# Block-causal attention with a SwiGLU layer on one core: the first microseconds rearranged

## The chip, the cores and the metric

The kernel runs on one core of a Trainium2 chip. The metric is device time in microseconds from the first to the last instruction of one execution, with what the launch adds around it; the median of several executions is compared. The engines are called PE (TensorE, with PEld for its weight loads), DVE (VectorE), ACT (ScalarE), POOL (GpSimd) and SP (SyncE, which here only issues transfers).

## The reference

Attention over 8 batches, 8 heads, 576 positions and a head dimension of 64, where a query sees the keys of its own block of 64 and of earlier blocks; the heads are then put side by side and go through a gated layer of widths 512, 1536 and 512. The weights of the layer arrive as 64-bit numbers.

```python
scores = scale * np.matmul(q, k.transpose(0, 1, 3, 2))
mask = block_i >= block_j                      # blocks of 64 positions
scores = np.where(mask, scores, -1000000000.0)
scores = scores - np.max(scores, axis=-1, keepdims=True)
attn = np.exp(scores)
attn = attn / (np.sum(attn, axis=-1, keepdims=True) + 1e-09)
x = np.matmul(attn, v)     # then as 4608 rows of 512
g = x @ w_gate
out = (g * (1.0 / (1.0 + np.exp(-g))) * (x @ w_val)) @ w_out
```

## The kernel before

The work is cut into tasks. `add(engine, cost, rank, fn, after, bufs)` records one: the engine, a planned cost, a rank, the function that emits its instructions, the tasks that it waits for and the buffers that it uses. `in_order()` then plays the tasks through a small model of five engines: whenever an engine is free, the ready task of lowest rank whose buffers are free goes next. The resulting list is emitted one task after the other, so each engine's program is that list in that order; what an instruction really waits for are its data and its buffers.

**Attention.** Scores are held with the keys on the partitions. Batches 0 and 1 are "early": each is cut into queries 0 to 255 and 256 to 575 (`FIRST`), and the eight heads go in four pairs. For a pair: `load_qk` brings q (SP) and k (ACT's queue for the very first four loads), `transposes` turn them on PE (L374) with `ident`, the 128x128 matrix of one, into the PSUM tiles `gv` or `at`; ACT copies them into `parts` (L382); `products` make the scores on PE (L400); ACT hides the unseen blocks (L441) and copies for the maximum (L444); DVE takes the maximum over key chunks into `mx` (L574); POOL reduces it over the partitions with PARTITION_ALL_REDUCE (L578); DVE subtracts it into `sc` (L602); ACT takes the exponent (L606); PE multiplies with `v` and with `ones` for the sums (L646). For the first 256 queries of batch 0, "tile 0", DVE inverts the sums (L673 to L677), multiplies (L680) and makes the low part (L297) of `xhl`, the input of the layer. There are four such inputs, one a pair.

**The layer.** The 4608 rows go in tiles of 256. `feed_forward` makes gate and value products on PE (L959 to L961; three products of high and low parts) into `gv`, and the down products (L1050 to L1052) into `po`. The weights come as pairs of 32-bit words: `weight(i, kind)` loads one block of gate, value or output weights (L812) into one of five `wo` buffers; ACT (L827) and DVE (L832, L836, L841) build 32-bit numbers from the words, and ACT and DVE split them into a high and a low part (L846, L849). There are 12 blocks of three kinds. The rank of a block's load is that of its other tasks: `R = 2.5 + i / 100.0 if i < 2 else 4.0 + i / 10.0`.

**Buffers.** PSUM has two `at`, two `gv` and one `po`; a task waits until the buffer that it writes is released. POOL fills the tiles of `v` and the tail of the keys in `parts` with zeros (L233, L211), and SP's first load into such a tile waits for that. `scratch` is the first `ob` tile, which ACT later uses for the weights' words.

**The matrix of one before:** on DVE, a row counting up is doubled in length seven times, turned for the partition's number, and compared (L271 to L279).

Of the kernel before, what the change touches and what calls it, by code (L numbers as in the profile page):

```python
# [9 lines left out]
I32 = mybir.dt.int32  # L10
AF = mybir.ActivationFunctionType
ALU = mybir.AluOpType
# [5 lines left out]
def kernel(  # L18
# [17 lines left out]
    nc = tc.nc  # L36
    B, H, S, D = q.shape
# [18 lines left out]
    MIXED = (0, 0, 0, 1, 1, 0, 1, 0, 1, 0, 1, 1)  # L56

    FINE = 4

    PATIENCE = 10.0  # L60

# [54 lines left out]
    class Task:  # L116
        def __init__(self, engine, cost, rank, fn, after, bufs, port, mode):
            self.engine, self.cost, self.rank, self.fn = engine, cost, rank, fn
            self.bufs, self.waits, self.next, self.ready = bufs, 0, [], 0.0
            self.moves, self.port, self.mode = 0.0, port, mode  # L120

            self.prev = None

    tasks = []

# [15 lines left out]
    def act_us(n):  # L141
        return 0.08 + n * 0.000833
# [4 lines left out]
    def mm_us(*ns):  # L147
        return sum(n / 2400.0 + 0.0145 for n in ns)


    def pair_us(*ns):
        return sum(n / 600.0 + 0.01 for n in ns)
# [113 lines left out]
            tiles_of(tag, place, variant)  # L266


    scratch = tiles_of("ob", 0)[0]
    count, mine = scratch[:, 0:P], scratch[:, P : P + 32]  # L270
    nc.vector.memset(count[:, 0:1], 0.0)  # L271
    for i in range(7):
        n = 2**i
        nc.vector.tensor_scalar(count[:, n : 2 * n], count[:, 0:n], float(n), None, ALU.add)
    nc.vector.transpose(mine, count[:, 0:32])
    for i in range(1, P // 32):
        rows = slice(32 * i, 32 * (i + 1))
        nc.vector.tensor_scalar(mine[rows, 0:1], mine[rows, 0:1], 32.0 * i, None, ALU.add)
    nc.vector.tensor_scalar(ident, count, mine[:, 0:1], None, ALU.is_equal)  # L279

    x_d = dram.tile([DM, NT], F32, name="x_d")
    s_d = dram.tile([H, NT], F32, name="s_d")
# [22 lines left out]
    def attention(R, b, h, a, e, early, bufs, lane):  # L305
# [35 lines left out]
        def plain_scores():  # L341
# [21 lines left out]
            for i in range(2):  # L363
                ps = Buf("gv") if whole else Buf("at", also=banks)
                nb = len(blocks[i])
                per = nb if nb < 6 else 3

                def turned(ps=ps):
                    return ps[0].rearrange("p (x n) -> p x n", x=1) if whole else ps[0]

                def transposes(i=i, turned=turned, per=per):
                    for m, c in enumerate(blocks[i]):
                        o = m % per * TB
                        nc.tensor.transpose(  # L374
                            turned()[:, m // per, o : o + TB],
                            qk[0][:TB, lane * 3 + c, 2 * i * D : 2 * (i + 1) * D],
                            ident[:TB, :TB],
                        )

                def out_of_psum(i=i, turned=turned, nb=nb, per=per):  # L380
                    o = L + blocks[i][0] * TB
                    nc.scalar.mul(  # L382
                        prt[i][:, o : o + nb * TB].rearrange("p (x n) -> p x n", x=nb // per),
                        turned()[:, 0 : nb // per, 0 : per * TB],
                        1.0 if i else SCALE,
                    )

                tr = add("PE", 0.083 * nb, R, transposes, [ld[i]], [qk, ps, prt])
                ready.append(add("ACT", act_us(nb * TB), R, out_of_psum, [tr], [ps, prt]))

            for visit in visits:
# [16 lines left out]

                ws = [w for parts in visit for _, _, w in parts]
                pr = add("PE", pair_us(*ws), Q, products, ready, [*both, prt, sc], mode="rows")  # L410
                for parts, ps in zip(visit, both):
                    gw = sum(w for _, _, w in parts)
                    mixed = [(c, sum(w for _, _, w in parts[:i])) for i, (c, qs, _) in enumerate(parts) if qs == c * P]
# [216 lines left out]
                    in_=v[b, h : h + 2, nf * P : e].rearrange("h p d -> p h d"),  # L630
                )

        vl = dma(R, 3e5, load_v, [], [vt], 3 if e % P else 2)
        segs = [s for s in ((0, 2 * P), (2 * P, S)) if a <= s[0] and s[1] <= e]
        ends = []
        direct = b == 0
# [146 lines left out]
    def weight(i, kind):  # L783
# [5 lines left out]


        R = 2.5 + i / 100.0 if i < 2 else 4.0 + i / 10.0
        raw = Buf("wo", "raw")
        away = AWAY.get(i) if kind == 2 else None
        wo = Buf("wo", "out") if kind == 2 and not away else None
# [16 lines left out]
                src = words(w_out)[i * P : (i + 1) * P, :].rearrange("p (n m) -> p n m", n=1)  # L811
            nc.sync.dma_start(out=view, in_=src)  # L812

        t = chain["w"] = dma(R, 5e5, load, [chain["w"]], [raw])
        bufs = [raw, wo] if wo else [raw]

        def words_of(j):
# [116 lines left out]
    def feed_forward(j, t0, w, xs):  # L934
# [41 lines left out]
        for i in range(0, NFC, 2):  # L976
# [65 lines left out]
            for piece in pieces:  # L1042
# [12 lines left out]
                after = [a, *(took[y][0] for y in ys), *{ends[m] for m in ms}]  # L1055
                bufs = [acc, hh, *(took[y][1] for y in ys if took[y][1])]
                t = add("PE", mm_us(DM, DM, DM) * len(piece), rank(i), products, after, bufs)
                for m in ms:
                    ends[m] = t
                if j >= FINE:  # L1060
# [21 lines left out]
    def with_v(rank):  # L1082
        us, products, after, bufs = zip(*(next(pair) for pair in at_work))
        t = add(
            "PE", sum(us), rank, lambda: [f() for f in products], sum(after, []), sum(bufs, []), mode="columns"
        )
        for pair in at_work:
            try:
                pair.send(t)
            except StopIteration:  # L1090
                pass
        at_work.clear()
# [44 lines left out]
    def in_order():  # L1137
# [42 lines left out]
        while events:  # L1180
# [3 lines left out]
            for e in engines:  # L1184
# [20 lines left out]
                order.append(t)  # L1205
                end = now + t.cost
                if e == "PE":
                    end, mode, last = end + 0.2 * (t.mode != mode), t.mode, t
                idle[e] = end
                heapq.heappush(events, end)  # L1210
# [20 lines left out]
    order = in_order()  # L1231
    with tc.manual_schedule():
        for t in order:
            t.fn()


# [26 lines left out]
```

## Time and profile before

| what | value |
|---|---|
| median of three executions | 1191.44 us (1189.01 to 1193.38) |
| the profiled execution | 1189.17 us |
| its span, first to last instruction | 1187.4 us |
| mean granted TensorE clock | 0.997 |
| PE busy | 1149.6 us, 97% |
| DVE, ACT, POOL busy | 772.0, 615.2, 322.6 us |
| PE idle for the matrix of one, at the start | 4.0 us |

An engine's busy time is summed over its instructions, so overlapping matmuls count once in a stretch. In a row of the timeline come start, length, engine, source line, operation, what it writes and reads, partitions and elements, the count, and in brackets how long the engine stood idle before it and for whom. A row with "x8" joins eight instructions; f32 products appear as two records each. Rows with SPq or ACTq are transfers being issued. In a table of stages the columns are the stretch, its length, each engine's busy time with its instructions in parentheses, the granted clock, the share of the transfer engines and GB/s.

### The profile page before, as it was taken

The numbers are of one execution on the slowest core, as the hardware profiler recorded it, in microseconds if no ns is written. First come the engines' busy times: TensorE is split into PE (matmuls) and PEld (weight loads), VectorE is DVE, ScalarE is ACT, GpSimd is POOL, SyncE is SP. The second block draws the span as 40 slices with busy tenths as digits, with TensorE's granted clock in tenths as the row PEclk, the third lists the DMA queues.
The fourth block names the chain that finished last, engine by engine and source line by source line (L and its number), as shares of the span: only waits on it lengthen the run. The fifth ranks groups of instructions, "written<-read, shape, count | busy, mean of one in ns | idle before, by whom it ended". The sixth has DMA issues, their size and how long they took to land.

```text
span 1187.4 us, 21716 instructions
## 1 busy us (share of the span) xinstructions
PE 1149.6 (97%) x8464; PEld 1028.4 (87%) x8464; DVE 772.0 (65%) x1269; ACT 615.2 (52%) x1114; POOL 322.6 (27%) x136
## 2 busy tenths in 40 slices
PE   6878999999999999999999999999999999999998
PEld 4647777888989899989898989898989899999997
DVE  5998998686768585957686768576767533323222
ACT  5777755675666655556555555474736312212111
POOL 3113001034544433324342425243253400000000
PEclk9999999999999999999999999999999999999999
DMA  7848765576556655665656556555652445454442
GB/s 182 243 117 231 208 181 170 162 226 162 156 145 180 177 145 160 180 192 159 174 167 185 148 155 167 183 147 183 166 182 97 155 162 172 158 166 136 142 137 94
DMA packets 266838, 197.39 MB, mean 166 GB/s; under 512 B 195248, under 2 KB 231104, under 8 KB 266736
## 3 DMA queue, kind: packets, MB, share of 16 engines
q1 hardware_dynamic: 264304, 195.42, 56.3%
q8 instruction: 66, 1.08, 0.4%
q10 hardware_dynamic: 2432, 0.59, 0.2%
q14 instruction: 36, 0.29, 0.1%
HBM read 171.57 MB, written 24.38 MB: 165 GB/s over the span
## 4 chain that ended last, share of the span: by engine, by line
PE 75%; DVE 0%; DMA 0%; ACT 0%; ACTq 0%; issue 0%; SPq 0%
PE gv L959 14%; PE gv L961 14%; PE gv L960 14%; PE po L1050 7%; PE po L1051 7%; PE po L1052 7%; PE at L526 6%; PE at L646 5%; DMA xt<-x_d 0%; DVE mx L574 0%; DVE parts L494 0%; DVE t L1000 0%; DVE hhl L1008 0%; ACT ob L1070 0%; ACTq L1259 0%
## 5 line engine op out<-in xcount | busy, mean ns | idle before, releaser
L578 POOL PARTITION_ALL_REDUCE mx<-mx x80 | 142.8, 1833 | 408.0 <-DVE mx L574 153.5
L959 PE MATMUL gv<-xhl,v_all 128*128 128x256 f32 x864 | 241.1, 279 | 0.4 <-DVE t L995 0.4
L961 PE MATMUL gv<-xhl,v_all 128*128 128x256 f32 x864 | 239.4, 277 | 0.0
L960 PE MATMUL gv<-xhl,v_all 128*128 128x256 f32 x864 | 239.2, 277 | 0.0
L697 POOL PARTITION_ALL_REDUCE mx<-mx x48 | 178.4, 3766 | 215.9 <-DVE mx L574 192.2
L995 DVE SCALAR_TENSOR_TENSOR t<-t,gv 128x512 f32<-128x512 f32 x108 | 74.0, 685 | 200.2 <-ACT t L992 199.4
L959 PEld LDWEIGHTS gv<-xhl,v_all 128*128 128x128 f32 x864 | 162.2, 188 | 3.2 <-issue 1.8
L960 PEld LDWEIGHTS gv<-xhl,v_all 128*128 128x128 f32 x864 | 162.3, 188 | 0.6
L961 PEld LDWEIGHTS gv<-xhl,v_all 128*128 128x128 f32 x864 | 162.2, 188 | 0.0
L1050 PE MATMUL po<-wo,hhl 128*128 128x512 f32 x396 | 157.0, 396 | 0.2 <-DMA wo<-wo_d 0.2
L1052 PE MATMUL po<-wo,hhl 128*128 128x512 f32 x396 | 154.5, 390 | 1.2 <-DVE hhl L1008 1.2
L1051 PE MATMUL po<-wo,hhl 128*128 128x512 f32 x396 | 155.0, 391 | 0.0
L992 ACT ACTIVATE t<-gv 128x512 f32<-128x512 f32 x108 | 64.7, 599 | 154.6 <-PE gv L961 154.0
L602 DVE TENSOR_TENSOR sc<-sc,mx 128x640 f32<-128x640 f32 (+6 forms) x168 | 124.6, 775 | 17.2 <-POOL mx L578 17.1
L1005 ACT CAST hhl<-t 128x512 fp32r<-128x512 f32 x108 | 67.1, 622 | 126.3 <-DVE t L1000 122.3
L1008 DVE TENSOR_TENSOR hhl<-t,hhl 128x512 fp32r<-128x512 f32 x108 | 94.9, 879 | 47.7 <-ACT hhl L1005 47.0
L606 ACT ACTIVATE sc<-sc 128x1024 f32<-128x1024 f32 (+3 forms) x104 | 105.4, 1029 | 39.0 <-DVE sc L602 37.9
L959 PE MATMUL gv<-xhl,g_even 128*128 128x256 f32 x432 | 123.3, 285 | 0.3 <-DVE t L1000 0.3
L961 PE MATMUL gv<-xhl,g_even 128*128 128x256 f32 x432 | 122.1, 283 | 0.0
L960 PE MATMUL gv<-xhl,g_even 128*128 128x256 f32 x432 | 122.1, 283 | 0.0
L959 PE MATMUL gv<-xhl,g_odd 128*128 128x256 f32 x432 | 121.4, 281 | 0.0
L961 PE MATMUL gv<-xhl,g_odd 128*128 128x256 f32 x432 | 119.7, 277 | 0.3 <-DVE g_odd L849 0.3
(155 smaller groups left out, 2393.6 us busy)
## 6 DMA issues: line engine op xcount, KB each, us to landing
wo<-wo_d SPq DMA_DIRECT2D x200, 512.0 KB
out_dram<-ob SPq DMA_DIRECT2D x36, 256.0 KB
v<-in_v_dram SPq DMA_DIRECT2D x64, 128.0 KB
xt<-x_d SPq DMA_DIRECT2D x64, 128.0 KB
rt<-r_d SPq DMA_DIRECT2D x128, 64.0 KB
qk<-in_q_dram SPq DMA_DIRECT2D x112, 72.0 KB
qk<-in_k_dram SPq DMA_DIRECT2D x104, 72.0 KB
x_d<-xu SPq DMA_DIRECT2D x24, 288.0 KB
```

Of the source, the lines that this page charges most:

```text
L578: nc.gpsimd.partition_all_reduce(m, m, channels=P, reduce_op=bass_isa.ReduceOp.max)
L602: nc.vector.tensor_tensor(piece(c), scores_of(c), m, ALU.subtract)
L606: nc.scalar.activation(x, x, AF.Exp)
L697: nc.gpsimd.partition_all_reduce(m, m, channels=P, reduce_op=bass_isa.ReduceOp.add)
L959: nc.tensor.matmul(o, lhsT=hi[:, d], rhs=xhi[:, 0:w], start=first, stop=False)
L960: nc.tensor.matmul(o, lhsT=hi[:, d], rhs=xlo[:, 0:w], start=False, stop=False)
L961: nc.tensor.matmul(o, lhsT=lo[:, d], rhs=xhi[:, 0:w], start=False, stop=last)
L995: nc.vector.scalar_tensor_tensor(t[0][:, 0:n], t[0][:, 0:n], 1.0, pg[0][:, 0:n], ALU.add, ALU.mult)
L1008: nc.vector.tensor_tensor(hh[1][:, 0:n], t[0][:, 0:n], hh[0][:, 0:n].bitcast(F32), ALU.subtract)
L1050: nc.tensor.matmul(po, lhsT=hi, rhs=whi, start=i + y == 0, stop=False)
L1051: nc.tensor.matmul(po, lhsT=hi, rhs=wlo, start=False, stop=False)
L1052: nc.tensor.matmul(po, lhsT=lo, rhs=whi, start=False, stop=i + y == NFC - 1)
```

## The change

Three things are done.

First, `ident` is made by GpSimd's `iota`, which writes column minus partition into `scratch`, and one comparison with zero on DVE. The chain of small DVE instructions goes.

Second, the ranks of loads change. `AHEAD` gives the first five weight loads ranks of 2.01 to 2.07 (only the load: the work on the weight keeps its rank), and early loads of v get a rank that is later by `LATER`.

Third, PE tasks of the first 90 planned microseconds carry in `over` the PSUM buffer that they will write, and where the plan has PE waiting, `fill` products of ones are emitted ahead of the task, into that same buffer. A fill is `ones` (128x64) times a broadcast column of ones (128x128). Their number is worked out from the planned wait. 94 are emitted, 48 of them ahead of tile 0's products.

The built program shows what this makes of the order. POOL from its first own instruction on, before and after; "ISA" without operands is the instruction that changes POOL's code to another set of operations, and the "ISA" with `mx` is the all-reduce:

```order
L233 MEMSET v_0_129 128x640
L211 MEMSET parts_1_153 128x64
L233 MEMSET v_0_160 128x640
L578 ISA
L578 ISA mx_0_181<-mx_0_181 128x256
L211 MEMSET parts_1_201 128x64
```

```order
L277 ISA
L277 IOTA ob_0_103 128x128
L240 MEMSET v_0_123 128x640
L218 MEMSET parts_1_152 128x64
L240 MEMSET v_0_184 128x640
L218 MEMSET parts_1_207 128x64
L579 ISA
L579 ISA mx_0_196<-mx_0_196 128x256 x4
```

The code is now changed twice, once for the iota at the very start and once for the all-reduce; the memsets stand between.

SP's first loads, before and after; `wo` is a weight buffer:

```order
L350 DMA qk_0_123<-in_q_dram 96x3x64 x2
L623 DMA v_0_129<-in_v_dram 128x2x64 x2
L350 DMA qk_0_123<-in_q_dram 96x3x64 x2
L623 DMA v_0_129<-in_v_dram 128x2x64 x2
L350 DMA qk_0_143<-in_q_dram 96x3x64 x2
L623 DMA v_0_160<-in_v_dram 128x2x64 x2
L350 DMA qk_0_143<-in_q_dram 96x3x64 x2
L623 DMA v_0_160<-in_v_dram 128x2x64 x2
L812 DMA wo_0_94<-in_moe_w_gate_dram 128x4x256
```

```order
L349 DMA qk_0_112<-in_q_dram 96x3x64 x2
L814 DMA wo_0_94<-in_moe_w_gate_dram 128x4x256
L349 DMA qk_0_112<-in_q_dram 96x3x64 x2
L624 DMA v_0_123<-in_v_dram 128x2x64 x2
L349 DMA qk_0_142<-in_q_dram 96x3x64 x2
L624 DMA v_0_123<-in_v_dram 128x2x64 x2
L814 DMA wo_0_95<-in_moe_w_val_dram 128x4x256
L349 DMA qk_0_142<-in_q_dram 96x3x64 x2
```

A gate block is now second and a value block seventh; q of the third and fourth pair (`qk_0_142`) stay behind loads of v.

PE around the fourth pair's scores and the first products with v, before and after; the fills are the rows with `ones` alone on the right:

```order
L646 MATMUL at_0_166<-sc_0_220,v_0_129 64x256 x2
L646 MATMUL at_0_166<-sc_0_220,v_0_129 64x128 x2
L646 MATMUL at_0_166<-sc_0_220,ones 64x256 x2
L646 MATMUL at_0_166<-sc_0_220,ones 64x128 x2
L400 MATMUL at_0_183<-parts_0_200,parts_1_201 128x256 x2
L400 MATMUL at_0_183<-parts_0_200,parts_1_201 128x128 x2
```

```order
L1247 MATMUL at_0_160<-ones 64x128 x6
L400 MATMUL at_0_160<-parts_0_206,parts_1_207 128x256 x2
L400 MATMUL at_0_160<-parts_0_206,parts_1_207 128x128 x2
L1247 MATMUL at_0_198<-ones 64x128 x5
L647 MATMUL at_0_198<-sc_0_248,v_0_123 64x256 x2
L647 MATMUL at_0_198<-sc_0_248,v_0_123 64x128 x2
L647 MATMUL at_0_198<-sc_0_248,ones 64x256 x2
L647 MATMUL at_0_198<-sc_0_248,ones 64x128 x2
L1247 MATMUL po_0_223<-ones 64x128 x2
```

The fourth pair's scores moved ahead of the first pair's products with v, and fills stand ahead of both; the first fills of all, eleven, are PE's very first instructions. The last two fifths of PE's order are the same as before.

The diff:

```diff
+    AHEAD = {(0, 0): 2.01, (0, 1): 2.01, (0, 2): 2.03, (1, 0): 2.05, (1, 1): 2.07}
+    LATER = 0.03
+    FILL = 90.0
...
-            self.prev = None
+            self.prev, self.over, self.fill = None, None, 0
...
-    scratch = tiles_of("ob", 0)[0]
-    count, mine = scratch[:, 0:P], scratch[:, P : P + 32]
-    nc.vector.memset(count[:, 0:1], 0.0)
-    for i in range(7):
-        n = 2**i
-        nc.vector.tensor_scalar(count[:, n : 2 * n], count[:, 0:n], float(n), None, ALU.add)
-    nc.vector.transpose(mine, count[:, 0:32])
-    for i in range(1, P // 32):
-        rows = slice(32 * i, 32 * (i + 1))
-        nc.vector.tensor_scalar(mine[rows, 0:1], mine[rows, 0:1], 32.0 * i, None, ALU.add)
-    nc.vector.tensor_scalar(ident, count, mine[:, 0:1], None, ALU.is_equal)
+    scratch = tiles_of("ob", 0)[0].bitcast(I32)[:, 0:P]
+    nc.gpsimd.iota(scratch, [[1, P]], channel_multiplier=-1)
+    nc.vector.tensor_scalar(ident, scratch, 0, None, ALU.is_equal)
...
                 tr = add("PE", 0.083 * nb, R, transposes, [ld[i]], [qk, ps, prt])
+                tr.over = ps
...
                 pr = add("PE", pair_us(*ws), Q, products, ready, [*both, prt, sc], mode="rows")
+                pr.over = both[0]
...
-        vl = dma(R, 3e5, load_v, [], [vt], 3 if e % P else 2)
+        vl = dma(R + (LATER if early else 0.0), 3e5, load_v, [], [vt], 3 if e % P else 2)
...
+        RL = AHEAD.get((i, kind), R)
-        t = chain["w"] = dma(R, 5e5, load, [chain["w"]], [raw])
+        t = chain["w"] = dma(RL, 5e5, load, [chain["w"]], [raw])
...
+                if i == 0 and piece[0] == (0, 0):
+                    t.over = acc
...
+        t.over = bufs[0][0]
...
                 if e == "PE":
+                    if t.over and now < FILL:
+                        if now < 8.0:
+                            t.fill = int(max(0.0, now - max(idle[e], 1.0)) / 0.213)
+                        elif now > idle[e] + 0.4:
+                            t.fill = int((now - idle[e]) * 0.6 / 0.107)
...
         for t in order:
+            for _ in range(t.fill):
+                o = t.over[0]
+                o = o[0:D, 0, 0:P] if t.over.tag != "gv" else o[0:D, 0:P]
+                nc.tensor.matmul(o, lhsT=ones, rhs=ones[:, 0:1].to_broadcast([P, P]), start=True, stop=True)
             t.fn()
```

## What is expected of it

> **What bounds the kernel now.** I read the engine summary first, then a table of stages, then the early waits engine by engine. The profiled execution took 1189.17 us around a span of 1187.4 us; the median of the runs is 1191.44 us, 2.3 us higher. I make the sum on 1189.2. Half a per cent of that, 6 us, is about what a measurement of this kernel can tell from no change. The stages (engines in the order PE, PEld, DVE, ACT, POOL; x counts instructions; then the granted TensorE clock):
>
> ```profile
> PE 1149.6 (97%) x8464; PEld 1028.4 (87%) x8464; DVE 772.0 (65%) x1269; ACT 615.2 (52%) x1114; POOL 322.6 (27%) x136
> 0.00:100.00 100.00, 76.31 (x555) 54.23 (x557) 80.99 (x177) 66.18 (x131) 23.87 (x26) 0.97 0.68 182
> 100.00:200.00 100.00, 93.81 (x700) 76.16 (x697) 91.68 (x167) 67.52 (x126) 14.77 (x13) 1.00 0.70 203
> 200.00:1187.00 987.00, 979.50 (x7215) 898.02 (x7213) 599.32 (x926) 481.53 (x857) 283.96 (x98) 1.00 0.55 161
> 0.00:10.00 10.00, 4.21 (x22) 3.03 (x22) 2.70 (x17) 3.65 (x8) 1.49 (x7) 1.00 0.68 153
> 10.00:20.00 10.00, 9.20 (x48) 6.53 (x50) 3.68 (x9) 5.74 (x12) 6.42 (x7) 1.00 0.96 244
> 20.00:30.00 10.00, 7.01 (x68) 5.07 (x65) 9.66 (x27) 6.75 (x12) 2.42 (x2) 1.00 0.54 151
> 30.00:40.00 10.00, 8.57 (x73) 6.06 (x73) 9.90 (x23) 9.79 (x21) 0.00 (x0) 1.00 0.92 253
> 70.00:80.00 10.00, 5.73 (x33) 3.15 (x35) 9.72 (x21) 7.79 (x14) 1.75 (x2) 0.89 0.52 149
> ```
>
> After 200 us PE idles 7.5 us of 987: that part is PE's own work and only its starting point can move. Before that PE idles 23.7 us in the first hundred and 6.2 in the second. From 20 us on DVE is the fuller engine (9.66, 9.90, 9.72 of 10), and in the first 20 it works 6.4. So an early microsecond counts if it brings DVE's saturated stretch forward, and I carry it whole to the end, because DVE and then PE are full behind it.
>
> The start: POOL's instruction that changes its code, then its timeline, then the rows of the chain that waits.
>
> ```profile
> L578 POOLq MODIFY_POOL_CONFIG  x2: 11/11/11, 2.0 to 2.1; - x2
> 0.73 0.63 POOL L233 MEMSET v<- 128x640 f32 x1 [0.29 <-POOLq L1246]
> 1.30 0.15 POOL L211 MEMSET parts<- 128x64 f32 x1
> 1.39 0.63 POOL L233 MEMSET v<- 128x640 f32 x1
> 10.95 1.06 POOL L578 PARTITION_ALL_REDUCE mx<-mx  x1 [8.93 <-DVE mx L574]
> 17.52 2.11 POOL L578 PARTITION_ALL_REDUCE mx<-mx  x2 [1.64 <-DVE mx L574]
> 23.44 2.42 POOL L578 PARTITION_ALL_REDUCE mx<-mx  x2 [3.81 <-DVE mx L574]
> 2.99 0.84 SPq L350 DMA_DIRECT2D qk<-in_q_dram  x2
> 6.19 0.84 SPq L350 DMA_DIRECT2D qk<-in_q_dram  x2
> 8.09 0.97 SPq L350 DMA_DIRECT2D qk<-in_q_dram  x2
> 1.20 1.68 DVE L274 TENSOR_SCALAR ob<-ob 128x1 f32<-128x1 f32 x6
> 3.62 0.28 DVE L279 TENSOR_SCALAR ident<-ob 128x128 f32<-128x128 f32 x1
> 3.96 1.22 PE L374 MATMUL gv<-ident,qk 96*128 96x96 f32 x6 [3.96 <-DVE ident L279]
> 6.51 0.71 PE L374 MATMUL gv<-ident,qk 96*128 96x96 f32 x3 [1.33 <-DMA qk<-in_q_dram]
> 9.98 1.65 PE L400 MATMUL at<-parts,parts 64*128 64x256 f32 x8 [0.50 <-ACT parts L382]
> 8.86 0.45 ACT L441 ACTIVATE at<-at,unseen 128x256 f32<-128x256 f32 x1 [1.18 <-PE at L400]
> 9.82 0.58 ACT L444 COPY mx<-at 128x512 f32<-128x512 f32 x1
> 10.44 0.42 DVE L574 TENSOR_TENSOR mx<-mx,at 128x256 f32<-128x256 f32 x1 [6.53 <-ACT mx L444]
> 13.59 1.01 DVE L602 TENSOR_TENSOR sc<-at,mx 128x512 f32<-128x512 f32 x2
> 16.64 1.55 PE L646 MATMUL at<-sc,v 128*64 128x256 f32 x8 [0.73 <-ACT sc L606]
> 17.95 1.52 PE L646 MATMUL at<-sc,ones 128*64 128x256 f32 x8
> 21.49 0.87 PE L646 MATMUL at<-sc,v 128*64 128x256 f32 x8 [1.03 <-DVE xt L680]
> 22.16 0.85 PE L646 MATMUL at<-sc,ones 128*64 128x256 f32 x8
> 36.76 0.41 DVE L297 TENSOR_TENSOR xhl<-xt,xhl 128x256 fp32r<-128x256 f32 x1
> ```
>
> The matrix of one, ready at 3.9 us, starts PE. The maxima of the first pair of heads reach POOL at 10.95. The last of tile 0's four inputs is done at 36.76 + 0.41 = 37.2 us, the mark that I follow below. POOL's change of code starts at 2.1 us, and its first all-reduce ran as soon as DVE was ready (10.44 + 0.42): the change is hidden, and lasts anything from 0 to 8.8 us. The products of L646 start 1.31 us apart at 16.64 and 0.67 apart at 21.49: PE's first 16 us run at half speed, though the granted clock reads 1.00 there.
>
> Half speed comes back twice, after pauses:
>
> ```profile
> 49.37 0.50 PE L1050 MATMUL po<-g_even,hhl 128*128 128x512 f32 x1 [3.44 <-ACT hhl L1005]
> 50.00:54.00 4.00, 4.00 (x11) 0.57 0.93 255
> 77.66 3.96 PE L646 MATMUL at<-sc,v 128*64 128x320 f32 x20 [2.73 <-ACT parts L382]
> 77.00:82.00 5.00, 4.34 (x26) 0.66 0.21 57
> 35.13 0.71 PE L374 MATMUL po<-ident,qk 96*128 96x96 f32 x6 [1.19 <-ACT sc L423]
> 35.68 0.99 PE L374 MATMUL at<-ident,qk 96*128 96x96 f32 x10
> ```
>
> Each time 4 x 0.43 and 5 x 0.34, that is 1.7 us of clock, are lost.
>
> **The change part by part.** *One fill.* Six transposes of 96 columns take 35.68 - 35.13 = 0.55 us, 0.95 ns a column. An f32 product stands in the trace as two such passes (four instructions of L646 give x8), so 128 columns cost 2 x 128 x 0.95 = 0.24 us; were passes on half of the columns to overlap, 0.12. I take 0.24, as all fills use the same half and follow each other; 0.48 at half speed.
>
> *Matrix of one.* DVE loses twelve instructions of set-up, 2.5 us up to 3.62. By themselves they are worth 0, since DVE idles until 10.44 anyway. POOL gains the iota and, ahead of it, a second change of code, because the iota is in another set than the all-reduce. The first load stands at 0.73 us; behind it wait the iota, the comparison, PE's transposes and, as POOL works in order, the memset of v, so SP's first load of v and every q load behind that. The second load comes after the memsets, ahead of the first all-reduce. Let one load take x, between 0 and 8.8. The nearest row is a transfer under this traffic: the q load issued at 2.99 let its transposes start at 6.51, 3.5 us. A change of code is two instructions (x2), so I take two such trips, x = 7.0, in the upper half of the bounds. The iota is between 0.13 (a fifth of the 0.63 memset, by elements) and 1.06 (an all-reduce); I take 0.3, by the memset. Then: iota done at 0.73 + 7.0 + 0.3 = 8.0, comparison 0.28, transposes from 8.4, 4.4 us later than now. Memsets 1.45, second load from 9.5 to 16.5: the first all-reduce starts there instead of at 10.95.
>
> *First loads.* SP issues weights second, seventh and eleventh instead of from the ninth on, and is then held at the v load until 8.6 us (iota 8.0, memset 0.63). q of the third pair follows near 9.6 (now 6.19), of the fourth near 12 (now 8.09): cost 0, since the all-reduces of the first two pairs hold POOL until 20.7. DVE's rows for the first gate and value weights move from after 21 us into its wait for POOL. In the built order DVE has done three whole weights and part of a fourth at the mark, before as after, so the relief shows only as far as DVE idles less up to there.
>
> *The start with x = 7.* Eleven first fills run from 1 us to 6.3 at the latest, under the load: 0. Pairs one to three have their scores by 15. All-reduces at 2.11 a pair: 16.5, 18.6, 20.7. The fourth pair's products wait for DVE to release their bank at 18.6 + 1.0 = 19.6; PE has then paused over 3 us, and by the row of 49.37 that brings half speed: six fills 2.9, products 1.6, until 24.1; ACT and DVE 0.45 + 0.58 + 0.42; its all-reduce at 25.6 (now 23.44). PE meanwhile: five fills 1.2 and pair one's products to 26.6; two fills and pair two to 28.4; the inversion on DVE 2.0 (from 17.95 + 1.52 to 21.49); ten fills behind the release of the bank, 2.4; pair three 1.3, to 34.1. From there 19 rows of DVE up to the mark, at 0.36 to 0.43 each (9.66 / 27, 9.90 / 23), make 7.3: 41.4 instead of 37.2, +4.2. With other x: below 6.4 the pause is too short for half speed, and 6.0 gives 36.5 (-0.7); 4.0 or less gives 32.5 (-4.7), from where PE's own chain holds it; 8.8 gives 41.4 + 2 x 1.8 = 45.0 (+7.8).
>
> *Later fills.* 46 follow. The 16 ahead of the first L1050 and the 14 ahead of the second large group of L646 stand in the waits of 3.44 and 2.73 us; they keep full speed, worth 2 x 1.7 = 3.4. The code counts fills for 0.6 of each planned wait at 0.107; at 0.24 they take 46 x 0.24 = 11.0 us in waits of 46 x 0.107 / 0.6 = 8.2, 2.8 over. Ends: -3.4 with the over-run hidden, +2.8 with no gain because DVE binds there (9.72 of 10). I take the clock and half of the over-run: -2.0.
>
> *Sum:* 1189.2 + 4.2 - 2.0 = 1191.4 us.
>
> **The rivals.** *Short loads.* With x of 4 or less the matrix comes near today's time, the four pairs' all-reduces stand close together, and DVE meets its weights early: 1189.2 - 4.7 - 2.0 = 1182.5, faster. For it: POOL shows no busy row during the change, and 4 is well inside the bounds. Against: two trips of 3.5 us.
>
> *Loads of 6.* Both loads are felt, but PE stays at full speed: 1189.2 - 0.7 - 2.0 = 1186.5, within half a per cent. This is what the Trainium skill (GPSIMD Engine Reference, Instruction dispatch) makes of it: the first call of a freshly loaded kernel pays about 6 us. The trace agrees as far as its bound of 8.8 goes; no row shows the load by itself.
>
> *The second load decides, slower.* At x = 8.8 the first all-reduce comes at 0.73 + 8.8 + 0.3 + 1.45 + 8.8 = 20.1 us, and while DVE binds later the regained clock buys nothing: 1189.2 + 7.8 = 1197.0. It ends slower from x = 7.9 up. For it: heavy traffic in those microseconds (0.68 and 0.96 of the DMA engines). Against: 8.8 is the longest that the trace allows.
>
> *The fills do not fill.* They write the bank that the next products use, so they start when it is released: behind a wait for the bank, not in it. 23 lie so in my start already. If the later ones do too, +2.8 and no clock: 1189.2 + 4.2 + 2.8 = 1196.2. For: every one of them names the bank of the product behind it. Against: the 16 write `po`, which nothing holds at that point.
>
> **How the numbers follow.** The forecast, loads of 6.4 to 7.9: 0.38, and loads of 4 to 6.4: 0.20, both within half a per cent. Short loads: 0.22, faster. The second load 0.12 and fills behind the waits 0.08: slower. The likeliest alone spans 1187 to 1195. To leave out no more than two in ten the range reaches to the rivals of both signs: 1182 to 1198.
>
> **What would show it.** Right: transposes on PE near 8.4 us; the first all-reduce near 16.5; the pairs' all-reduces nearly back to back; no half clock near 50 and 77; tile 0's last input near 41. Wrong: transposes before 6, which is the short load; a first all-reduce near 20; or PE's 29.9 us of idle time in the first 200 changed by more than 6, which would mean that the early stage carries to the end otherwise than I think.

## The result, and the profile after

The changed kernel takes 1213.68 us (median; 1211.54 to 1216.72) beside 1191.88 us of the kernel before, run with it. The ratio is 1.018, with a 95% interval of 1.016 to 1.020: 21.8 us slower between the medians. The forecast was 1191.4 us, and the range ended at 1198. The profiled execution took 1216.72 us around a span of 1214.9 us, 27.5 us more than that of before.

The changed kernel's summary of the engines:

```profile
PE 1177.7 (97%) x8652; PEld 1057.9 (87%) x8652; DVE 784.0 (65%) x1257; ACT 615.6 (51%) x1114; POOL 327.0 (27%) x137
```

Its stages, in the windows that were shown of before (PE, PEld, DVE, ACT, POOL, then the granted clock):

```profile
0.00:100.00 100.00, 85.23 (x655) 70.57 (x655) 68.11 (x140) 55.59 (x106) 22.56 (x25) 0.95 0.62 163
100.00:200.00 100.00, 91.49 (x660) 71.39 (x661) 88.15 (x163) 67.72 (x130) 18.48 (x14) 0.98 0.66 189
200.00:1187.00 987.00, 977.40 (x7185) 894.59 (x7184) 621.88 (x948) 488.11 (x871) 285.98 (x98) 1.00 0.55 162
```

PE is busy 28.1 us longer, and its idle time has not shrunk: 1214.9 - 1177.7 = 37.2 us, beside 1187.4 - 1149.6 = 37.8. Over the whole span, what was added to fill waits stands beside the waits. DVE does less in the first hundred (68.1 us instead of 81.0).

Its first load of code begins, by the line that asks for it (first and last start last), at

```profile
L277 POOLq MODIFY_POOL_CONFIG  x2: 11/11/11, 0.8 to 0.8; - x2
```

The timelines of POOL, SP, DVE and PE at the start (start, busy time, and in brackets the idle time ahead with its releaser):

```profile
8.74 0.23 POOL L277 IOTA ob<- 128x128 int32 x1 [8.32 <-issue]
8.94 0.62 POOL L240 MEMSET v<- 128x640 f32 x1
17.23 5.00 POOL L579 PARTITION_ALL_REDUCE mx<-mx  x4 [6.92 <-DVE mx L575]
9.59 0.91 SPq L624 DMA_DIRECT2D v<-in_v_dram  x2
10.54 0.97 SPq L349 DMA_DIRECT2D qk<-in_q_dram  x2
9.01 1.38 DVE L278 TENSOR_SCALAR ident<-ob 128x128 f32<-128x128 int32 x1 [7.87 <-POOL ob L277]
0.97 4.96 PE L1247 MATMUL gv<-ones 128*64 128x128 f32 x22 [0.97 <-DVE ones L170]
10.45 1.22 PE L373 MATMUL gv<-ident,qk 96*128 96x96 f32 x6 [4.52 <-DVE ident L278]
41.48 0.42 DVE L296 TENSOR_TENSOR xhl<-xt,xhl 128x256 fp32r<-128x256 f32 x1
```

So that load lasts from 0.8 to 8.7 us. The matrix of one follows at 10.4, the first all-reduce at 17.23, and the mark, tile 0's last input, comes at 41.48 + 0.42 = 41.9 us: 4.7 later than before. The other 23 us of the span are lost behind the mark.

The fills behind 40 us in PE's timeline, group by group (two instructions are one fill), and ACT's exponentials ahead of the third group:

```profile
44.75 1.11 PE L1247 MATMUL at<-ones 128*64 128x128 f32 x4 [2.19 <-ACT parts L381]
57.05 3.77 PE L1247 MATMUL po<-ones 128*64 128x128 f32 x32
73.03 1.47 ACT L607 ACTIVATE sc<-sc 128x768 f32<-128x768 f32 x2
74.81 4.85 PE L1247 MATMUL at<-ones 128*64 128x128 f32 x27 [2.21 <-ACT sc L424]
79.39 0.48 PE L647 MATMUL at<-sc,v 128*64 128x320 f32 x1
84.78 0.88 PE L1247 MATMUL at<-ones 128*64 128x128 f32 x6 [0.50 <-ACT parts L381]
92.70 1.21 PE L1247 MATMUL at<-ones 128*64 128x128 f32 x9 [0.90 <-ACT sc L424]
101.35 1.54 PE L1247 MATMUL at<-ones 128*64 128x128 f32 x12 [0.53 <-DVE xt L681]
```

A bracket at a fill's own row is a pause in which PE stood still because the fill waited for its bank: 2.19 + 2.21 + 0.50 + 0.90 + 0.53 = 6.3 us in these rows. Only the group on `po` starts with no pause ahead of it. At 74.81 the exponentials that the next products read were ready (73.03 + 1.47 = 74.5) and their bank was just free; the products came at 79.39, behind 4.6 us of fills, most of them at half speed (the granted clock is 0.72 from 74 to 80 us). The group on `po` starts in a wait, but outlasts it: the products behind it need ACT's `hhl`, and they start at 60.75.

```profile
57.88 0.62 ACT L1007 CAST hhl<-t 128x512 fp32r<-128x512 f32 x1 [1.16 <-DVE t L1002]
60.75 0.50 PE L1052 MATMUL po<-g_even,hhl 128*128 128x512 f32 x1
```

That input was done at 57.88 + 0.62 = 58.5, 2.2 us before.

### The profile page after: what moved, and what is told of

Same layout as the page of the kernel before. It is cut to its first block, busy times and chain, and to the rows that moved or that the text cites. A ratio compares the mean times of both kernels' runs of the same rounds, so it can differ in the third digit from the quotient of the medians.

```text
span 1214.9 us, 22082 instructions
## 1 busy us (share of the span) xinstructions
PE 1177.7 (97%) x8652; PEld 1057.9 (87%) x8652; DVE 784.0 (65%) x1257; ACT 615.6 (51%) x1114; POOL 327.0 (27%) x137
## 4 chain that ended last, share of the span: by engine, by line
PE 82%; DVE 4%; DMA 4%; ACT 4%; issue 3%; SPq 1%; POOL 1%; ACTq 0%; POOLq 0%; DVEq 0%
PE gv L961 15%; PE gv L962 14%; PE gv L963 14%; PE at L647 7%; PE po L1052 7%; PE po L1053 7%; PE po L1054 7%; PE at L527 6%; DMA wo<-in_moe_w_val_dram 1%; PE at L1247 1%; PE at L400 1%; DMA wo<-in_moe_w_out_dram 1%; ACT sc L607 1%; DVE mx L575 1%; POOL mx L579 1%
## 5 line engine op out<-in xcount | busy, mean ns | idle before, releaser
L579 POOL PARTITION_ALL_REDUCE mx<-mx x80 | 144.2, 1849 | 440.8 <-DVE mx L575 194.9
L698 POOL PARTITION_ALL_REDUCE mx<-mx x48 | 181.2, 3823 | 198.2 <-DVE mx L575 171.6
L603 DVE TENSOR_TENSOR sc<-sc,mx 128x640 f32<-128x640 f32 (+6 forms) x168 | 127.2, 793 | 15.8 <-POOL mx L579 15.5
L1010 DVE TENSOR_TENSOR hhl<-t,hhl 128x512 fp32r<-128x512 f32 x108 | 100.0, 926 | 49.6 <-ACT hhl L1007 48.9
```

The lines of the kernel that those rows point to most:

```text
L579: nc.gpsimd.partition_all_reduce(m, m, channels=P, reduce_op=bass_isa.ReduceOp.max)
L603: nc.vector.tensor_tensor(piece(c), scores_of(c), m, ALU.subtract)
L698: nc.gpsimd.partition_all_reduce(m, m, channels=P, reduce_op=bass_isa.ReduceOp.add)
L1010: nc.vector.tensor_tensor(hh[1][:, 0:n], t[0][:, 0:n], hh[0][:, 0:n].bitcast(F32), ALU.subtract)
```

## The experiments

Differences in us below are between medians of kernels that ran on the same chip, with the ratio and its 95% interval. A ratio of 1.005 is 6 us.

**One part taken out of the changed kernel.**

```diff
a_no_fills:   -            for _ in range(t.fill):
              +            for _ in range(0):
a_dve_ident:  the twelve DVE instructions for `ident` are back, the iota is out
a_old_loads:  -    AHEAD = {(0, 0): 2.01, ...
              +    AHEAD = {}
              -    LATER = 0.03
              +    LATER = 0.0
```

> The changed kernel with no fill emitted; iota and new loads stay, and the order is the same, since the fills never entered the plan. Theory F (fills run behind the release of the bank, so they cost their own time: 29.2 us of PE in the changed trace, 5.0 of them under the first load of code): 1213.7 less about 15, so 1196 to 1202. Theory I (the two code loads move the whole start, ident at 10.4 instead of 3.9 us, and that carries to the end): a few us at most, 1210 to 1214, or even slower, since the clock is no longer kept up. Theory R (the new order of loads makes the plan worse): 1210 to 1214.

> The changed kernel with the matrix of one made on DVE as before; fills and new loads stay. Theory I: ident back near 4 us, the first all-reduce near 11 to 12, and 5 to 7 us saved, 1206 to 1209; all of the 22 us if the loads were the whole cause, 1192. Theory F: the eleven first fills, hidden under the load until now, would end near 6 us and so stand 2 us behind the matrix; 1209 to 1214. Theory R: 1208 to 1214.

> The changed kernel with the old ranks of the loads (no early weights, v not later); iota stays, fills stay but their number follows the plan. Theory R: 1195 to 1203. Theories F and I: 1210 to 1216.

Measured against the kernel before: without fills 1.0109 [1.0083, 1.0135], with DVE's matrix 1.0136 [1.0117, 1.0154], with the old ranks 1.0139 [1.0120, 1.0159]. Their medians are 1207.35, 1208.82 and 1209.39 us. Against 1.0179 each part takes off 0.4 to 0.7%, none all of it: three separate losses. The matrix came in theory I's 1206 to 1209, a range that overlaps that of R. For the fills and for the ranks no theory had the time: it fell between the ranges.

PE's rows of `a_no_fills` show what the fills displaced. These are the products that stand behind the groups of 74.81, 84.78 and 92.70 in the changed kernel:

```profile
69.61 2.28 PE L647 MATMUL at<-sc,v 128*64 128x320 f32 x20 [2.21 <-ACT sc L424]
74.84 1.13 PE L400 MATMUL at<-parts,parts 64*128 64x320 f32 x8 [0.50 <-ACT parts L381]
82.64 2.27 PE L647 MATMUL at<-sc,v 128*64 128x320 f32 x20 [0.90 <-ACT sc L424]
```

Without fills the products wait as long as the fills did, and for the same releaser: 2.21, 0.50 and 0.90 us. So these three groups filled nothing; they took the place of products that could have started.

**One part alone in the kernel before.** These are the same edits the other way round; in the old order the plan puts 121 fills instead of 94.

> The kernel before with the fills alone (121 by this plan; matrix on DVE, old loads). Theory F, read from the three runs so far (taking them out of the changed kernel saved 6.3 us): 1197 to 1201, the early lag growing from place to place where fills stand behind a released bank. Rival (the fills only cost in company of the new order): 1189 to 1194.

> The kernel before with the new ranks of the loads alone: matrix of one on DVE, no fills. Theory R: 1200 or more. If the order is harmless and F and I hold the loss between them: 1187 to 1193, and a little faster than before if weights under the first waits of DVE help (up to 4 us).

> The kernel before with the iota alone. Theory I: transposes near 10.4 us, the first all-reduce near 17, and a lag that stays about 4 to 6 us: 1196 to 1199. If DVE's saturated stretch takes the late start up: 1192 to 1194. With only_loads at +8.6, plain addition to the changed kernel's +21 leaves 12 for fills and iota together.

| alone | us | before | ratio | difference |
|---|---|---|---|---|
| fills (121 in the old order) | 1202.77 | 1192.43 | 1.0084 [1.0067, 1.0100] | +10.3 |
| ranks of the first loads | 1201.35 | 1192.77 | 1.0076 [1.0058, 1.0093] | +8.6 |
| iota and one comparison | 1198.69 | 1192.43 | 1.0051 [1.0032, 1.0069] | +6.3 |

`only_fills` came out above the 1197 to 1201 expected, the other two within their ranges. The sum, 25.2 us, is somewhat above the 21 to 22 of all together. The rest of the runs take the three one by one.

**The iota: the matrix, SP's queue, or the second load?** `idle_iota` adds an iota to the kernel before that nobody reads; `iota_v_dve` also gives the memsets of `v` to VectorE, so that SP's loads no longer stand behind POOL.

```diff
 idle_iota:
+    spare = tiles_of("ob", 1)[0].bitcast(I32)[:, 0:P]
+    nc.gpsimd.iota(spare, [[1, P]], channel_multiplier=-1)
     scratch = tiles_of("ob", 0)[0]
 iota_v_dve, besides:
-    pool_of(const, "v", 2, ..., lambda t: nc.gpsimd.memset(t, 0.0))
+    pool_of(const, "v", 2, ..., lambda t: nc.vector.memset(t, 0.0))
```

> The kernel before, with an iota that nothing reads as POOL's first work: both code loads, but the matrix of one still comes from DVE near 4 us. If a load takes what the first one took in the changed kernel (8.0 us from 0.7 to 8.7), the second ends at 10.3 + 8.0 = 18 and the first all-reduce starts there; if it was shorter than the 6.9 us that it had in the changed kernel, near 16 or earlier. Total: if the loss of the iota comes through the late all-reduces and loads of v, about that of only_iota; if it comes through the late matrix, 1191 to 1194.

> The kernel before with an iota on GpSimd that nobody reads, and with the two memsets of v moved from GpSimd to VectorE; the matrix of one is still made by VectorE. It tells the two paths of the iota's cost apart. Theory Q (the first load of code holds the memset of v, so SyncE's loads of v and of q behind it): without that the second q load is issued at about 3 us again, its transposes start near 6.5, the maxima of the first pair reach VectorE's end near 10.9 as before, and what is left is the second load of code: begun behind the iota at about 8.6 us, it puts the first all-reduce at 8.6 + 8.0 = 16.6 if it lasts as long as the first, so that only about 1 us of the 6.4 comes back, 1198. Rival L2 (the second load is short, since the first included the start of the program): the all-reduce at 12 or earlier, and the time 1193 to 1194. Rival O (the cost has nothing to do with the first 17 us): no change of either, 1199, with the all-reduce early.

`idle_iota`: 1199.04 beside 1192.43, 1.0053 [1.0035, 1.0071]. Its timelines of DVE, SP, PE and POOL:

```profile
3.13 0.28 DVE L281 TENSOR_SCALAR ident<-ob 128x128 f32<-128x128 f32 x1
9.98 0.97 SPq L352 DMA_DIRECT2D qk<-in_q_dram  x2
13.06 0.71 PE L376 MATMUL gv<-ident,qk 96*128 96x96 f32 x3 [7.96 <-DMA qk<-in_q_dram]
17.53 1.08 POOL L580 PARTITION_ALL_REDUCE mx<-mx  x1 [7.89 <-DVE mx L576]
```

The matrix is as early as ever and the loss is the whole +6.6, as large as with the late matrix (+6.3): in this order of loads the late matrix cost nothing that these runs can tell. The second q load is issued at 9.98 us instead of 2.99, because SP waits at the load of `v` for POOL's memset, and that memset stands behind the load of code. `iota_v_dve`: 1194.62 beside 1191.75, 1.0022 [1.0013, 1.0031]. Its second change of code on POOL begins at

```profile
L580 POOLq MODIFY_POOL_CONFIG  x2: 7/7/7, 9.2 to 9.3; - x2
```

and the rows of its timelines that answer to the last three are

```profile
3.05 1.01 SPq L352 DMA_DIRECT2D qk<-in_q_dram  x2
10.27 0.42 DVE L576 TENSOR_TENSOR mx<-mx,at 128x256 f32<-128x256 f32 x1 [5.68 <-ACT mx L446]
15.06 1.08 POOL L580 PARTITION_ALL_REDUCE mx<-mx  x1 [6.05 <-issue]
```

With SP free, q is on time, and the first all-reduce is held by nothing but its own load of code: "issue" is the releaser, and 9.2 to 15.06 makes 5.9 us for the second load. So of the +6.6, freeing SP's queue from POOL's memset takes off 3.7, and 2.9 are left, which these rows put down to the second load. (The two runs had different chips, and the intervals leave 2 us of doubt to the split; VectorE's two memsets are in the 2.9.) The expectation had 8 us for it and 1198 us, and its rival an all-reduce by 12 and at most 1194. Neither came: the load is shorter than the first (7.9), and too long to hide. The Trainium skill (GPSIMD Engine Reference, Instruction dispatch) gives about 6 us for the load of a fresh kernel; the second load here agrees, the first, at the start of the program, does not.

Both runs have the old order of loads. In the changed kernel the first two q loads go out ahead of the first `v` (the second at 2.18 us), and the first all-reduce stands behind the matrix instead: from 10.45, when the matrix is there, PE works without a pause through the transposes and six fills to the products at 14.09. In `a_no_fills` these products come at 12.21 and the first all-reduce at 16.53.

**The ranks of the loads.** Both were set; `only_ahead` has the weights ahead alone, `only_later` the v loads later alone, which moves no weight forward.

```diff
 only_ahead:   AHEAD as in the change, LATER = 0.0
 only_later:   no AHEAD,
-        vl = dma(R, 3e5, load_v, [], [vt], 3 if e % P else 2)
+        vl = dma(R + (LATER if early else 0.0), 3e5, load_v, [], [vt], 3 if e % P else 2)
 late_replan:  AHEAD = {(8, 0): 6.5}, LATER = 0.0
```

> The kernel before with the five weight loads ranked ahead and nothing else (the v loads keep their rank). Theory T (the cost of the new order of loads is one of the transfers: weights ahead of q and v hold them up): all of the +8.6 us of both ranks together is here, 1200 to 1202, and the other half alone is at 1192. Theory R (the planner walks its list anew, and what is lost is lost by an order that suits the engines less, beyond 200 us, with TensorE pausing and losing clock): an amount of its own, anywhere from 1190 to 1203, with the marks of the first 60 us within 3 us of the kernel before, and the two halves not adding up to +8.6.

> The kernel before with the first v loads ranked 0.03 later and nothing else: no weight load is moved ahead. Theory T: no change, 1191 to 1194, since no transfer is put ahead of one that the start waits for. Theory R: this too makes the planner walk its list anew, and the time is another by some us in either direction, 1188 to 1203, with the difference arising beyond the first 60 us.

> The kernel before with one rank changed: the gate weights of block 8 get 6.5 instead of 4.8, which leaves the first hundred loads of SyncE and the first 240 instructions of VectorE word for word as they are, and makes the planner set a new order from there on (about 90 us) to the end. Theory R (what the new ranks cost is the worse fit of a new order, not the loads that they move): a cost or gain of some us here too, 1194 to 1203 the likelier, with equal start times up to 85 us. Theory E (the cost comes from what the first 60 us look like): within 1.5 us of the kernel before, 1190 to 1193.

`only_ahead` 1200.81 (1.0072 [1.0051, 1.0093], +9.1), `only_later` 1204.25 (1.0094 [1.0068, 1.0121], +12.5), both beside 1191.75; `late_replan` 1197.82 beside 1192.33 (1.0043 [1.0028, 1.0057], +5.5). The halves make 21.6, the two together 8.6, as theory R had it and theory T had not; `only_later` is even above R's 1203. And in `only_later` the start is early, not late: by the start of the n-th all-reduce in either trace it leads the kernel before by 0.3 to 6.6 us up to 81 us, and trails by 2.6 us and more from 200 on. (Its traced execution, 1198.46 us, is the fastest of five, so the trace holds about half of the loss.) PE from 200 to 400 us (length, busy, clock), first in the kernel before:

```profile
200.00:400.00 200.00, 196.47 (x1440) 1.00 0.61 172
```

and then in the changed kernel:

```profile
200.00:400.00 200.00, 191.38 (x1372) 0.98 0.59 165
```

Idle time and lost clock there (200 less the busy time, and 200 times what the clock lacks) from the same row of each kernel:

| order | kernel | busy | clock | idle and lost |
|---|---|---|---|---|
| as before | the kernel before | 196.47 | 1.00 | 3.5 |
| as before | `only_iota` | 196.80 | 1.00 | 3.2 |
| new | `only_loads` | 192.04 | 0.99 | 10.0 |
| new | `only_ahead` | 193.71 | 0.98 | 10.3 |
| new | `only_later` | 192.94 | 0.99 | 9.1 |
| new | `late_replan` | 194.22 | 0.98 | 9.8 |
| new | the changed kernel | 191.38 | 0.98 | 12.6 |

The other kernels that keep the order lose 3.4 us there (`iota_v_dve`) to 6.0 (`only_fills`), the other two with the new order 9.1 (`a_no_fills`) and 11.2 (`a_dve_ident`). The clock has two decimals, so the last column is good to about 1 us. `only_ahead` and `only_later` lose another 3.5 and 5 us between 110 and 200 us.

PE's waits in these 200 us (total, times, longest): the longest in the kernel before,

```profile
PE po L1052 <- DVE hhl L1008: 1.2, 1, 1.2
```

and the two longest in the changed kernel:

```profile
PE gv L961 <- DVE t L1002: 3.0, 1, 3.0
PE po L1054 <- DVE hhl L1010: 1.9, 1, 1.9
```

The four runs show new orders that cost 5.5 to 12.5 us, whatever the loads do early. `late_replan`, whose products of the feed-forward part start within 1.5 us of those of before up to 124 us, shows that nothing early is needed for it. Nor is it the moved load: the last load of weights goes out at 195.84 us there and at 198.04 before, and none of PE's waits from 200 to 400 us is for weights. The expectation had the order new to the end; it is not. Compared row by row, the traces of PE, DVE and ACT differ from 136 to 756 us in `late_replan`, up to 392 in `only_ahead`, up to 756 in the others, and agree behind that. Which pair of rows in the new orders makes each wait was not followed up, and four orders do not show that every order would lose.

**The fills: where they stand and how long.** In the kernel before: `po_fills` has only the 19 ahead of the first L1050, `first_fills` only the 19 planned before 8 us, `late_fills` only the other 102, `short_fills` all 121 over 32 columns, `best_fills` the first 19 and 11 ahead of L1050.

```diff
 po_fills:     tr.over, pr.over and t.over = bufs[0][0] are not set
 first_fills:  -  elif now > idle[e] + 0.4:
               +  elif False:
 late_fills:   -  t.fill = int(max(0.0, now - max(idle[e], 1.0)) / 0.213)
               +  t.fill = 0
 short_fills:  -  rhs=ones[:, 0:1].to_broadcast([P, P])
               +  rhs=ones[:, 0:1].to_broadcast([P, 32])
 best_fills:   -  t.fill = int((now - idle[e]) * 0.6 / 0.107)
               +  t.fill = 11 if t.down else 0     # t.down: the first piece of L1050
```

> The kernel before with the 19 fills ahead of the first down products alone; they write po, which nothing holds there, in a wait of 3.44 us. Theory F in its full form (what counts is whether the bank is free during the wait): half speed at 50 us gone, 1.7 us of clock back, less 19 x 0.23 = 4.4 in 3.4 of wait: 1190 to 1193, no change that can be told. Rival (any fill costs its time): 1195 to 1197.

> The kernel before with only those fills that are planned before 8 us (19 of them, ahead of the first transposes and products). Theory W (full speed from the start shortens the chain of the first pairs): the products of the first pairs in half their time, the first all-reduce 1 to 2 us earlier, 1190 to 1191. Theory F (the chain there is one of transfers, ScalarE, VectorE and GpSimd, and the fills beyond the first wait stand in PE's way, 8 of them by 0.23 to 0.48 us): the first all-reduce at its place within 0.5 us, the time 1192 to 1195.

> The kernel before with the fills planned after 8 us (102 of the 121 of this order) and without the 19 earlier ones. The 19 alone took 2.4 us off (1189.36 beside 1191.75), the 121 together cost 10.3. Theory S (each fill has a price of its own place): the 102 cost 10.3 + 2.4 = 12.7, 1203 to 1206, and the start is as in the kernel before (first all-reduce 10.9). Rival (the early ones only pay or cost together with the later ones, through the clock): 1198 to 1202.

> The kernel before with the same 121 fills at the same places, each over 32 columns instead of 128. Theory B (the price is TensorE's time behind the released bank, 121 fills of 0.23 us): a fill becomes about a quarter, 0.06 us; 102 x 0.17 = 17 us of TensorE's time fall away, and the time comes to 1191 to 1195. Rival K (the price is one of the bank itself or of the order: a product that must wait until the writes before it have left, whatever their length): still 1199 to 1203.

> The kernel before with the 19 fills planned before 8 us, and 11 instead of 19 fills ahead of the first products of the down projection: 11 x 0.233 = 2.6 us in a wait of 3.1. If the early fills' gain of 2.4 us and a regained clock of 1.7 us stand beside each other: 1187 to 1189, and no half speed near 50 us. If VectorE binds there and the clock buys nothing: 1189 to 1190, as with the 19 alone.

| fills | us | before | ratio |
|---|---|---|---|
| `po_fills` | 1191.80 | 1192.43 | 0.9996 [0.9983, 1.0009] |
| `first_fills` | 1189.36 | 1191.75 | 0.9978 [0.9967, 0.9989] |
| `late_fills` | 1204.48 | 1192.33 | 1.0100 [1.0082, 1.0118] |
| `short_fills` | 1205.95 | 1192.33 | 1.0107 [1.0090, 1.0124] |
| `best_fills` | 1190.16 | 1192.33 | 0.9982 [0.9973, 0.9990] |

The first 19 gain 2.4 us and the later 102 lose 12.1; together they make the +10.3 within its interval. The time of `late_fills` came as expected; `first_fills` came out below both of its ranges, `best_fills` just above the higher of its two. The start of `first_fills` in the timelines of PE and POOL:

```profile
0.99 4.51 PE L1255 MATMUL gv<-ones 128*64 128x128 f32 x22 [0.99 <-DVE ones L170]
8.04 0.92 PE L408 MATMUL at<-parts,parts 64*128 64x256 f32 x8
10.84 1.06 POOL L587 PARTITION_ALL_REDUCE mx<-mx  x1 [8.82 <-DVE mx L583]
16.60 2.11 POOL L587 PARTITION_ALL_REDUCE mx<-mx  x2 [1.48 <-DVE mx L583]
22.01 2.42 POOL L587 PARTITION_ALL_REDUCE mx<-mx  x2 [3.31 <-DVE mx L583]
```

The products of a pair take 0.92 us instead of 1.65, so the fills have brought PE to full speed. The first all-reduce gains only 0.1 us: the fills hold the first transposes until 5.42 us (3.96 before), and the full speed no more than makes that good. The last starts 1.4 us earlier than its 23.44 of before. My expectation F had the first all-reduce right; theory W had the halved products and the sign of the time.

The fills ahead of the down projection in `po_fills`:

```profile
46.70 4.43 PE L1252 MATMUL po<-ones 128*64 128x128 f32 x38
51.06 0.50 PE L1058 MATMUL po<-g_even,hhl 128*128 128x512 f32 x1
```

The same place in `best_fills`, and what comes 8 us later:

```profile
44.03 2.66 PE L1255 MATMUL po<-ones 128*64 128x128 f32 x22
48.06 0.50 PE L1060 MATMUL po<-g_even,hhl 128*128 128x512 f32 x1 [1.38 <-ACT hhl L1015]
59.67 2.34 PE L408 MATMUL at<-parts,parts 64*128 64x320 f32 x12 [2.90 <-DVE xt L689]
```

PE in two windows of `best_fills` (length, busy, clock):

```profile
45.00:56.00 11.00, 9.62 (x70) 1.00 1.00 284
56.00:65.00 9.00, 6.10 (x38) 0.81 0.23 69
```

and of the kernel before:

```profile
45.00:56.00 11.00, 7.56 (x35) 0.84 0.98 277
56.00:65.00 9.00, 7.34 (x67) 1.00 0.41 115
```

The half speed near 50 us goes away with 19 fills and with 11. With 19 the down projection starts 1.7 us late, though only 0.6 of it is the fills' doing: ACT's `hhl`, which it reads, was done at 50.42 instead of 49.32, as ACT stood behind a load of weights that landed later. With 11 it is not late, PE runs ahead, waits 2.90 us for DVE at 59.67, and loses there (9 x 0.19 = 1.7 us) what it kept before (11 x 0.16 = 1.8). As these rows read, DVE sets the pace there, and the regained clock moved the pause; no run makes DVE faster to test it.

`short_fills` missed its expectation, 1191 to 1195, and the rival's 1199 to 1203 too. I had left the clock out. A group and the products behind it in `late_fills`, 128 columns:

```profile
66.86 2.44 PE L1255 MATMUL at<-ones 128*64 128x128 f32 x20 [1.67 <-DVE xt L689]
69.22 1.57 PE L408 MATMUL at<-parts,parts 64*128 64x320 f32 x12
```

The same in `short_fills`, 32 columns, and its group on `po`:

```profile
51.65 2.40 PE L1255 MATMUL po<-ones 128*64 128x32 f32 x38
65.27 1.99 PE L1255 MATMUL at<-ones 128*64 128x32 f32 x20 [2.44 <-DVE xt L689]
67.19 2.93 PE L408 MATMUL at<-parts,parts 64*128 64x320 f32 x12
```

The pauses ahead differ too (1.67 and 2.44 us), so this pair alone does not show that the fills' length makes the half speed. From 8 to 110 us the fills of `only_fills`, the same 121, are busy for 26.7 us at a clock of 1.00, those of `short_fills` for

```profile
8.00:110.00 102.00, 18.76 (x210) 0.90 0.60 164
```

The short fills save 8.0 us of PE's time and lose, by estimate, up to 102 x 0.10 = 10.2 us of clock. The two balance, so this run does not decide between TensorE's time and a price of the bank. For the time speak the rows of the changed kernel at 74.81 and of `po_fills`, in which the products start exactly at the fills' end. Fills into another bank than that of the next product were not tried.

No version beats the kernel before by more than `first_fills`, 0.22%. `best_fills` is the same within the intervals.

## Why the prediction was wrong, step by step

**First loads, cost 0: +8.6 alone.** This is the step that failed in kind. The new ranks were judged by the rows up to the mark at 37 us, and up to there they were harmless (in `only_loads` the first eight all-reduces start within -0.6 to +2.2 us of before). But the planner had laid a new order up to 756 us, and most of the loss is in 200 to 400 us. The first part of the prediction said that after 200 us "only its starting point can move"; that holds for a kept order (3.2 to 6.0 us lost there, 3.5 before), not for a new one (9 to 13). Which rows of the new order make the loss stays open.

**Later fills, -2.0: a loss.** In the old order those behind 8 us cost 12.1; taking all 94 out of the changed kernel saves 0.7%, 6 to 8 us. No run has the 46 of this term alone. The rival "the fills do not fill" had the mechanism, and I gave it 0.08. Its price, +2.8, took the waits' planned size as cover; in the trace the bank is released at the end of the wait, so most of the fill is added. The argument against it, that the fills on `po` find a free bank, was right for that one group (57.05), which then outlasted its wait by 2.2 us, and wrong as a ground for the other five. The clock came back at one of the two places: 1.00 from 57 to 66 us, around the down products, but 0.72 from 74 to 80, and 0.71 from 45 to 56, where it had read 0.84 before. Where it did come back, worth 1.7 us on paper, it bought nothing, as `po_fills` and `best_fills` show: of my bounds, +2.8 with no gain "because DVE binds there" was the nearer, and it was too low.

**First fills, 0.** In the kernel before they gain 2.4 us, and the all-reduces put the gain at the later pairs, not the first. In the changed kernel the 0 was right in effect: the eleven fills end 4.5 us before the transposes, which then take 1.22 us for six, half speed again. The first all-reduce comes at 17.23 with fills and at 16.53 in `a_no_fills`, the last two at 26.86 and 26.76.

**The start, +4.2.** The mark came at 41.9 beside 41.4 forecast, the first all-reduce at 17.23 beside 16.5, the all-reduces of the first pairs back to back: right as numbers, and partly by luck, for the way was another. I took a load of 7.0 for both; they are 7.9 and 5.9. In my sum the second load holds the first all-reduce. In the changed kernel its row at 17.23 names DVE, and what holds DVE is the late matrix (transposes at 10.45, not 8.4, partly because the comparison took 1.38 us, not 0.28) with the six fills behind it. The half speed that I had at the fourth pair did not come either (its six fills took 1.54 us at 21.79, not 2.9). The term in the sum was too small by 2, by the iota alone (+6.3). That run has the old order of loads, and there "cost 0" for the q loads behind `v` failed: q behind POOL's memset decides the first all-reduce, about 3.7 of 6.6 us are its, and the late matrix cost nothing. In the changed kernel DVE's matrix gives back 0.43%, 5 us; how they divide between matrix and loads of code was not tried.

**What would make it wrong.** I had named a change of PE's idle time in the first 200 by more than 6 us. It went from 29.9 to 23.3, 6.6 less, and this was no gain: the fills count as busy. The test should have been on PE's time without fills.

## What to carry to other kernels

A filler instruction fills a wait only if it needs nothing that the wait is for, and only if it is done when the wait ends. Look in the order at which buffer it writes and who holds it, and read the bracket at its own row: a pause ahead of the filler means that it starts when the real work could. Where a planner lays the order, a change of one number can be a new program for hundreds of microseconds behind it (here up to 756), and is to be read in the late stages too. An instruction moved to GpSimd is paid at everything that stands behind it on GpSimd's and then on SyncE's queue, and at the change of code back.

## What the runs showed of the hardware that I had not expected

The first load of code ended 7.9 us after its instruction (0.8 to 8.7), the second, in the middle of the program, 5.9. The comparison that makes `ident` took 1.38 us from an int32 tile, 0.28 from a float one of the same size (1.28 in `only_iota`); GpSimd's memsets ran beside the slow one, and which of the two slows it was not tried. Fills over 32 columns take 0.063 us a pass in `short_fills` (2.40 us for the 38 on `po`) instead of 0.117 (4.43 us for 38 in `po_fills`), both at a granted clock of 1.00: half and not a quarter. Over 8 to 110 us PE is busy for 90.4 us with them and 90.7 with the long ones of `only_fills`, yet the clock is 0.90 beside 1.00; why stays open. The Trainium skill (TensorE: Matmul & The Clock Gate, Part 1) says that full speed comes after one busy window of about 3.4 us; the long fills at the start of `first_fills` agree with that: they follow each other every 0.21 us up to 4.7 us and every 0.11 from 4.9, 3.9 us after the first. It is no fixed time: in the changed kernel the first 22 passes keep to 0.21 for all of their 5.0 us. The short ones in `short_fills`, over 2.6 us there, left the six transposes behind them at 1.22 us, as before.
